# A spectral transform and two MLPs on one core: y's partial sums added as they leave PSUM, the first MLP's drain and the second MLP's first block laid out by hand

## The chip, the cores and the metric

The kernel runs on one core of one Trainium2 chip. The metric is device time in microseconds (us) of one execution, the median of three runs. The engines are named as in the profile: PE is TensorE (matmuls; PEld its weight loads), DVE is VectorE, ACT is ScalarE, POOL is GpSimd, SP is SyncE, whose queue issues every transfer here. Each engine works through its own queue in order; semaphores order the engines among each other.

## The reference, cut to what matters

```python
def reference(x, moe_w_in, moe_w_out, moe2_w_in, moe2_w_out):
    # x: (2, 3008, 256); w_in: (256, 2048); w_out: (2048, 256)
    y = np.fft.fft(np.fft.fft(x, axis=1), axis=2).real.astype(np.float32).reshape(6016, 256)
    r = np.maximum(y @ moe_w_in, 0.0)                  # first MLP
    y = ((r * r) @ moe_w_out).astype(np.float32)
    h = y @ moe2_w_in                                  # second MLP
    g = h * (1.0 / (1.0 + np.exp(-1.702 * h)))
    return (g @ moe2_w_out).astype(np.float32)
```

The weights come as 64-bit floats.

## The kernel before

**Numbers in two parts.** A float32 operand of a matmul is split into a high part (a cast to fp32r) and a low part (the operand less its high part), and a product is made of three matmuls: high by high, high by low, low by high. So nearly every operand costs one cast on ACT and one subtraction (the helper `sub`, line 78) on DVE or POOL. A 64-bit weight is narrowed to 32 bits first: `narrow` (from line 165) is six operations for a group of 1024 columns, two on ACT (lines 171, 174 or their like) and four on DVE (lines 175, 176, 185, 187).

**First stage.** x is folded by symmetry, transformed along the features and along the tokens, and stands as eight blocks j = 0 to 7 of 376 or 378 columns; a column is a pair of tokens, and each block has an even and an odd part.

**First MLP.** It runs in 128 steps i, listed in `steps`; a step is one block j and one slice f of 128 of the 2048 hidden features. `turns` gives the order: blocks 0, 1 and 2 are made in several turns, because the weights are narrowed meanwhile (block 0 in slices 0 to 4 and 4 to 16, block 1 in 0 to 4, 4 to 12 and 12 to 16, block 2 in 0 to 8 and 8 to 16), blocks 3 to 7 in one turn of 16. In a step `front1` makes six matmuls into a tile of the pool `psa` (two banks, two buffers). DVE turns them into h (lines 742, 744, 745: p, then two halves of h), ACT does relu, square and the cast to gh (lines 751, 752, 754), and POOL, in some steps DVE, subtracts gl a step later (line 78). The tile h has the tag "h" with four buffers. Four steps later (`LAG`) `back` multiplies gh and gl by the second weights: twelve matmuls, six for each output half ec = 0, 1, into the accumulators `acc[j]`, two tiles of the pool `psb`, which has just two buffers. At a turn's last step `store` copies both accumulators out, ec 0 on ACT and ec 1 on DVE (line 582), into tiles o that also have the tag "h", and sends them to a DRAM tile of that turn (line 583). So blocks 0, 1 and 2 leave two or three partial sums of y in DRAM. Outside of the parts written under `manual_schedule`, a scheduler in the compiler sets the order of each engine's queue from the program's order, so the order in the trace is not line by line that of the source.

Beside the steps run jobs of a plan (`PLAN`, `background`): the later parts of the transform, the narrowing of the weights, and at the end "y0" (from step 111, due at 128). That is `y_first`: `add_y(0)` loads the further partial sums of the first 512 columns and adds them on DVE (line 638), `sums_y` makes four differences of y's quarters (line 647), and `stage_a` and `stage_b` split y and these into yA and yB (ACT casts at line 654, DVE subtractions at line 78). yA may use a weight buffer that is free from step 117, yB one that is free from step 121.

**Second MLP.** y stands in six blocks of 512 columns (the last has 452), and a block is made in eight units p, so units u = 0 to 47. A unit multiplies by a two-by-two scheme with seven products: `products` (line 792) makes yb and ya's four into the PSUM tiles ab and cd, then, after DVE and ACT have formed u and g[3] from them (lines 839, 842, 843, 844), yc's three into the same tiles. DVE adds (line 868), ACT applies the activation (lines 867, 869) and casts gh a unit later (line 847), DVE subtracts gl. Two units later `back2` (line 808) multiplies by the output weights, half of it (ec 0) between the unit's first and second products, half (ec 1) after them. Its accumulators are `psb` tiles too. All of this is written under `manual_schedule`: the order of each engine's queue is the order of the source.

In units 0 and 1 the place of `back2` is taken by the drain: the last four steps' `back` (`drain`), two a unit. At u = 2 `leave` (lines 811 to 814) copies block 7's accumulators out, ec 0 on ACT and ec 1 on DVE, both through the one buffer of the tag "o" in the pool m3. Meanwhile a generator, `w2_late` (`rest`), is advanced by a number of pieces at three places in a unit. It narrows the last four groups of the second MLP's weights (input weights of group 2, output weights of group 2, then group 3 of each), loads y's block 1, adds its partial sums on DVE (`add_y(1)`) and makes its differences on DVE. For input weights `widen_in` makes four sums on POOL (line 234), four casts on ACT (line 242) and four subtractions on POOL (line 78). All narrowing goes through one buffer (`temp(cv2)`), the tile ue.

Input weights of group 2 are needed from u = 4, output weights of group 2 from u = 6, the next input group from u = 6, the next output group from u = 8. At the last unit of a block (`turn`) the next block's yB, yA and yC are made. At the very end the last accumulator leaves by two copies and two transfers (lines 891 to 896), again through the one buffer "o".

## Time and profile before

| what | value |
|---|---|
| three timed runs, us | 1013.51, 1017.29, 1017.41 (median 1017.29) |
| the profiled execution, us | 1017.06, of which the span from first to last instruction is 1015.3 |
| busy share of the span | PE 96%, weight loads 85%, DVE 70%, ACT 59%, POOL 32% |
| mean granted TensorE clock | 0.987 of full speed |
| end of the first MLP's last step on PE | 483.1 us after the span's start |
| first block of the second MLP (u = 0 to 7) | 483.1 to 590.9 us |

The profile is one execution. Its page gives shares of the whole span; what a stage is worth is read from its stretch: the busy time of each engine there, the clock that was granted, and which wait ended last before an engine went on. The rows below are in this form: a timeline row has the start, the duration, the engine, the line, the operation, the tile written and the tiles read, and in brackets how long the engine had stood idle before and what ended that.

### The profile page before, as it was taken

What the parts mean: (1) busy time and instruction counts of PE and PEld (TensorE: products, weight loads), DVE (VectorE), ACT (ScalarE), POOL (GpSimd) and SP (SyncE); (2) the same over time, 40 slices, a digit from 0 to 9 for tenths busy, and PEclk for the clock granted to TensorE, in tenths of its full rate; (3) what the DMA queues carried; (4) which work ended last, traced back from release to release, by engine and by line L of the source; (5) the groups of instructions that cost most, each with busy time, mean ns of one, the idle gap of its engine ahead of it and who ended that gap; (6) DMA issues with size and microseconds to landing.
All of it is one profiled execution on the core that took longest, in us unless ns stands there. A gap on an engine that the chain in (4) does not pass through costs nothing.

```text
span 1015.3 us, 12479 instructions
## 1 busy us (share of the span) xinstructions
PE 971.1 (96%) x4862; PEld 857.9 (85%) x4862; DVE 707.3 (70%) x881; ACT 599.7 (59%) x688; POOL 320.4 (32%) x200
## 2 busy tenths in 40 slices
PE   9889988999999999999779899999999999999997
PEld 8579988998999899999657688888888888888896
DVE  6996887885978787878656776575565556556552
ACT  2588887766676668787645454454454445445442
POOL 2367687534575457665223002020001001000000
PEclk9999999999999999999889999999999999999999
DMA  7640221300101001120211202002002000000101
GB/s 291 212 156 36 92 95 42 103 29 27 42 32 42 31 8 66 42 84 1 83 48 67 83 25 87 1 1 83 0 1 78 1 1 21 21 0 1 42 1 37
DMA packets 23675, 53.58 MB, mean 53 GB/s; under 512 B 3776, under 2 KB 17216, under 8 KB 20928
## 3 DMA queue, kind: packets, MB, share of 16 engines
q1 hardware_dynamic: 23616, 52.79, 15.1%
q8 instruction: 38, 0.62, 0.2%
q14 instruction: 21, 0.17, 0.1%
HBM read 37.36 MB, written 15.42 MB: 52 GB/s over the span
## 4 chain that ended last, share of the span: by engine, by line
PE 67%; DVE 7%; ACT 3%; issue 1%; DMA 1%; POOL 1%; DVEq 0%; ACTq 0%
PE psb L808 24%; PE psc L792 21%; PE psb L469 14%; PE psa L454 2%; PE psa L456 2%; PE psa L455 2%; PE psa L353 1%; POOL w2i L78 1%; DVE gl L78 1%; DVE h L744 1%; DVE ue L647 1%; DVE p L742 1%; DVE h L745 1%; DVE ue L185 1%; DMA ydram<-o 0%
## 5 line engine op out<-in xcount | busy, mean ns | idle before, releaser
L78 POOL TENSOR_TENSOR gl<-h,gh 128x752 fp32r<-128x752 f32 (+1 forms) x118 | 222.8, 1892 | 161.2 <-ACT gh L754 129.2
L469 PE MATMUL psb<-gh,w 128*128 128x376 f32 (+1 forms) x1024 | 239.2, 336 | 0.7 <-DVE o L582 0.7
L808 PE MATMUL psb<-gh,w 128*128 128x512 f32 (+1 forms) x768 | 223.5, 393 | 5.8 <-ACT o L813 5.8
L469 PEld LDWEIGHTS psb<-gh,w 128*128 128x128 f32 x1024 | 183.2, 189 | 1.9 <-issue 1.0
L808 PEld LDWEIGHTS psb<-gh,w 128*128 128x128 f32 x768 | 146.0, 190 | 36.7 <-ACT o L813 6.2
L868 DVE TENSOR_TENSOR g<-u,psc 128x1024 f32<-128x1024 f32 (+1 forms) x48 | 57.6, 1200 | 123.7 <-PE psc L792 123.7
L751 ACT ACTIVATE h<-h 128x752 f32<-128x752 f32 (+1 forms) x114 | 94.8, 832 | 65.3 <-DVE h L745 61.4
L469 PE MATMUL psb<-gl,w 128*128 128x376 f32 (+1 forms) x512 | 130.5, 336 | 0.0
L869 ACT ACTIVATE g<-g 128x1536 f32<-128x1536 f32 (+1 forms) x48 | 70.4, 1467 | 98.1 <-DVE g L868 98.1
L754 ACT CAST gh<-h 128x752 fp32r<-128x752 f32 (+1 forms) x128 | 105.0, 822 | 31.6 <-DVE h L749 24.7
L808 PE MATMUL psb<-gl,w 128*128 128x512 f32 (+1 forms) x384 | 121.0, 397 | 2.6 <-DVE gl L78 2.6
L792 PE MATMUL psc<-yc,w2i 128*128 128x512 f32 (+1 forms) x432 | 106.3, 389 | 4.3 <-DVE u L842 2.7
L78 DVE TENSOR_TENSOR gl<-g,gh 128x2048 fp32r<-128x2048 f32 (+1 forms) x48 | 108.8, 2266 | 2.1 <-ACT gh L847 1.2
L742 DVE SCALAR_TENSOR_TENSOR p<-n,w1n_t,psa 128x376 f32<-128x376 f32 (+1 forms) x128 | 76.4, 600 | 37.1 <-PE psa L456 36.6
L792 PEld LDWEIGHTS psc<-yc,w2i 128*128 128x128 f32 x432 | 80.6, 188 | 23.4 <-DVE u L842 4.3
L752 ACT ACTIVATE h<-h 128x752 f32<-128x752 f32 (+1 forms) x114 | 94.9, 834 | 3.1
L647 POOL TENSOR_TENSOR ue<-raw 128x512 f32<-128x512 f32 (+1 forms) x8 | 9.9, 1263 | 270.7 <-DVE yc L78 200.4
L454 PE MATMUL psa<-eo,w 128*128 128x376 f32 (+1 forms) x256 | 88.4, 346 | 6.6 <-DVE p L742 3.4
L469 PEld LDWEIGHTS psb<-gl,w 128*128 128x128 f32 x512 | 93.2, 190 | 0.0
L847 ACT CAST gh<-g 128x2048 fp32r<-128x2048 f32 (+1 forms) x48 | 90.1, 1876 | 0.1
L808 PEld LDWEIGHTS psb<-gl,w 128*128 128x128 f32 x384 | 72.6, 190 | 19.2 <-DVE gl L78 4.2
L455 PE MATMUL psa<-eo,w 128*128 128x376 f32 (+1 forms) x256 | 85.9, 336 | 0.0
(126 smaller groups left out, 1373.0 us busy)
## 6 DMA issues: line engine op xcount, KB each, us to landing
ydram<-o SPq DMA_DIRECT2D x18, 376.0 KB, 2.9
xt<-in_x SPq DMA_DIRECT2D x5, 1024.0 KB, 5.7
out<-o SPq DMA_DIRECT2D x10, 512.0 KB, 2.6
cst<-in_dfts SPq DMA_DIRECT2D x8, 570.0 KB, 5.6
raw<-in_w1i SPq DMA_DIRECT2D x4, 1024.0 KB, 4.9
raw<-in_w1o SPq DMA_DIRECT2D x4, 1024.0 KB, 6.2
raw<-in_w2i SPq DMA_DIRECT2D x4, 1024.0 KB, 4.9
raw<-in_w2o SPq DMA_DIRECT2D x4, 1024.0 KB, 5.0
```

What stands on the lines that cost most here:

```text
L78: eng.tensor_tensor(out=o, in0=a, in1=f32(b), op=ALU.subtract)
L454: T.matmul(o, lhsT=w[:, 0, fs], rhs=t[:, par, 0, 0:wd], start=True, stop=False)
L455: T.matmul(o, lhsT=w[:, 0, fs], rhs=t[:, par, 1, 0:wd], start=False, stop=False)
L469: T.matmul(acc[j][ec][:, s, 0:wd], lhsT=w[:, hl, e0:e0 + P], rhs=(gh, gl)[gi][:, s, 0:wd], start=(first and hl == 0 and gi == 0), stop=(la ...
L742: V.scalar_tensor_tensor(out=p[:, 0:wd], in0=e128[blocks[j]][:, 0:wd], scalar=w1n_t[:, 0, f:f + 1], in1=ps[:, 0, 0:wd], op0=ALU.mult, op1= ...
L751: A.activation(out=hv, in_=hv, func=AF.Relu)
L752: A.activation(out=hv, in_=hv, func=AF.Square)
L754: last_a = A.copy(gh[:, :, 0:wd], hv)
L792: T.matmul(bank, lhsT=w[:, hl, slot * P:(slot + 1) * P], rhs=x[:, yl, 0:wd], start=(first and hl == 0 and yl == 0), stop=(hl == 1), skip_g ...
L808: T.matmul(o[:, s, 0:wd], lhsT=w[:, hl, e0:e0 + P], rhs=g[:, 2 * i + s, 0:wd], start=(f == 0 and hl == 0 and g is gh), stop=(f == 15 and h ...
L847: A.copy(gh, gs[u - 1])
L869: A.activation(out=g[:, 1:4], in_=g[:, 1:4], func=AF.Gelu_apprx_sigmoid)
```

## The change

- `store` adds: where an earlier turn's sum of the block exists, the new function `ahead`, called one step before, loads it into two tiles o of the tag "h", DVE adds the accumulator onto each, and the sum goes out. So each block has one y in DRAM. `add_y` is removed, and `load_y` always reads one tensor a block; y's blocks after the first all come to raw buffer 1.
- `y_first` begins with `sums_y`. The differences of block 1 are made on POOL instead of DVE.
- The drain is halved by output: unit 0 makes ec 0 of all four last steps, unit 1 makes ec 1. Block 7's ec 0 leaves at u = 1 into a buffer of its own (`spare`), its ec 1 at u = 2.
- `w2_late` no longer is a generator: its pieces are put into a table by unit and place in the unit (0, 1 and 2 before yc's products, "m" between the two activations), and `do_late` issues them. The low halves of the input weights are made on DVE, the output weights are narrowed in a buffer of their own, and the last output group's narrowed weights go to raw buffer 0.
- The last output leaves through a buffer of the tag "g", and a small tile "edge" is allocated that nothing uses.

```diff
@@ -456,13 +456,13 @@
             T.matmul(o, lhsT=w[:, 1, fs], rhs=t[:, par, 0, 0:wd], start=False, stop=True)
         return pq
 
-    def back(j, f, first, last):
+    def back(j, f, first, last, ecs=range(2)):
         wd = WID[blocks[j][1]]
         if first:
             acc[j] = [ps_b(), ps_b()]
-        gh, gl = gst.pop((j, f))
+        gh, gl = gst[j, f]
         w = weights[0, 1, f // 4]
-        for ec in range(2):
+        for ec in ecs:
             e0 = (f % 4) * 256 + ec * P
             for hl, gi in ((0, 0), (0, 1), (1, 0)):
                 for s in range(2):
@@ -571,16 +571,30 @@
                     gone.add(name)
             assert name in gone, name
 
+    leaving = {}
+
+    def ahead(j):
+
+        wd = WID[blocks[j][1]]
+        leaving[j] = [m.tile([P, 2, NP], F32, tag="h", name="o", bufs=4) for _ in range(2)]
+        for ec, o in enumerate(leaving[j]):
+            nc.sync.dma_start(o[:, :, 0:wd], ydram[j][:, ec, :, 0:wd])
+
     def store(j, f):
 
         wd = WID[blocks[j][1]]
+        before = j in ydram
         y = dram.tile([P, 2, 2, NP], F32, tag=f"y{j}_{f}", name="ydram")
-        ydram.setdefault(j, []).append(y)
+        ydram[j] = y
+        o2 = leaving.pop(j, None)
         for ec in range(2):
-            o = m.tile([P, 2, NP], F32, tag="h", name="o", bufs=4)
             ap = acc[j][ec][:, :, 0:wd]
-            (A.copy, V.tensor_copy)[ec](o[:, :, 0:wd], ap)
-            nc.sync.dma_start(y[:, ec, :, 0:wd], o[:, :, 0:wd])
+            o = (o2[ec] if before else m.tile([P, 2, NP], F32, tag="h", name="o", bufs=4))[:, :, 0:wd]
+            if before:
+                V.tensor_tensor(out=o, in0=o, in1=ap, op=ALU.add)
+            else:
+                (A.copy, V.tensor_copy)[ec](o, ap)
+            nc.sync.dma_start(y[:, ec, :, 0:wd], o)
 
     pend = None
     n = len(steps)
@@ -602,40 +616,9 @@
         return tl[:, 0:4 * NP2].rearrange("p (e s k) -> p e s k", e=2, s=2)
 
     def load_y(m):
-        yr[m] = f32(quarters(raw_tile(m % 2)))
+        yr[m] = f32(quarters(raw_tile(1 if m else 0)))
         for j, lo, hi, at in pieces(m):
-            nc.sync.dma_start(yr[m][:, :, :, at:at + hi - lo], ydram[j][0][:, :, :, lo:hi])
-
-    def add_y(m):
...
     def sums_y(m, eng):
         wd = WID2[m]
@@ -678,23 +661,11 @@
             else:
                 yield from widen(1, 1, g, cv2, dest, then=then)
 
-    def w2_late():
-        then = ((lambda: load_w(1, *order[6], slot=1)), (lambda: load_w(1, *order[7], slot=0)), (lambda: load_y(1)), None)
-        yield lambda: load_w(1, *order[5], slot=0)
-        for i in range(4):
-            k, g = order[4 + i]
-            if k == 0:
-                yield from widen_in(g, temp(cv2), (winp, wq), then=then[i])
-            else:
-                yield from widen(1, 1, g, cv2, (winp, wq)[g - 2], then=then[i])
-        yield from y_next(1)
-
     def until(i):
         while at_step[0] < i:
             yield lambda: None
 
     def y_first():
-        yield from add_y(0)
         yield from sums_y(0, V)
         yield from until(117)
         yA[0] = view(winp.tile([P, 2, 1024], F32R, tag="w", name="ya"), 2)
@@ -704,12 +675,90 @@
         yield from stage_b(0)
 
     def y_next(m):
-        if m > 1:
-            load_y(m)
-            yield lambda: None
-            yield lambda: None
-        yield from add_y(m)
-        yield from sums_y(m, G if m > 1 else V)
+        load_y(m)
+        yield lambda: None
+        yield lambda: None
+        yield from sums_y(m, G)
+
+    late = {}
+
+    def put(u, spot, *items):
+        late.setdefault((u, spot), []).extend(items)
+
+    def in_parts(g, ue, tiles):
...
+        return sums, highs, lows
+
+    def out_parts(g, u, w):
+        weights[1, 1, g] = w
+        return lambda: A.copy(w[:, 0], u), lambda: sub(V, w[:, 1], u, w[:, 0])
+
+    def w_tile(pool, dtype=F32R):
+        return pool.tile([P, 2, 1024], dtype, tag="w", name="w2")
+
+    def w2_late():
+
+        load_w(1, *order[5], slot=0)
+        in2, spare, out2, in3 = (w_tile(winp), w_tile(wq)), w_tile(wq, F32), w_tile(winp), (w_tile(winp), w_tile(wq))
+        ue = temp(cv2)
+        p = list(narrow(raws[1, 0, 2], ue, (1, 0, 2)))
+        sums, highs, lows = in_parts(2, ue, in2)
+        put(0, 1, *p, lambda: load_w(1, *order[6], slot=1), *sums)
+        put(1, 1, *highs, *lows)
+
+        def out_2():
+            p = list(narrow(raws[1, 1, 2], spare, (1, 1, 2)))
+            put(1, "m", *p[:2])
+            put(2, 1, *p[2:], lambda: load_w(1, *order[7], slot=0))
+            put(3, 1, *out_parts(2, spare[:, 0], out2))
+
+        def in_3():
+            ue = temp(cv2)
+            p = list(narrow(raws[1, 0, 3], ue, (1, 0, 3)))
+            sums, highs, lows = in_parts(3, ue, in3)
+            p[0]()
+            p[1]()
+            put(3, 1, *p[2:5], lambda: load_y(1))
+            put(4, 1, p[5], *sums)
+            put(5, 1, *highs, *lows)
+
+        def out_3():
+            p = list(narrow(raws[1, 1, 3], spare, (1, 1, 3)))
+            for item in p[:4]:
+                item()
+            put(5, 0, p[4])
+            put(6, 1, p[5])
+
+        def out_3_end():
+            high, low = out_parts(3, spare[:, 0], raw_tile(0, F32R).rearrange("p (h c) -> p h c", h=2))
+            high()
+            put(7, 1, low)
+
+        put(1, 0, out_2)
+        put(2, 2, in_3)
+        put(4, 2, out_3)
+        put(6, 1, lambda: run(sums_y(1, G)))
+        put(6, "m", out_3_end)
+        return spare
+
+    def do_late(u, spot):
+        for f in late.get((u, spot), ()):
+            f()
 
     held = []
     by_hand = ExitStack()
@@ -726,6 +775,8 @@
             zp.release()
             w2b = tc.alloc_tile_pool(name="w2b", bufs=3, side="left", reuse_waits="tile")
         at_step[0] = i
+        if LAG <= i + 1 < n and steps[i + 1 - LAG][4] and steps[i + 1 - LAG][1] in ydram:
+            ahead(steps[i + 1 - LAG][1])
         j, f = steps[i][1:3]
         ps = front1(j, f)
         done = steps[i - LAG][1:] if i >= LAG else None
@@ -781,7 +832,8 @@
     yC[0] = m2.tile([P, 2, 3, NP2], F32R, tag="yc", name="yc")
     units = 8 * BLKS
     run(stage_c(0))
-    rest = w2_late()
+    rest = None
+    spare = w2_late()
     drain = [steps[n - LAG + k][1:] for k in range(LAG)]
     gs, gsp = {}, {}
 
@@ -808,8 +860,9 @@
                     T.matmul(o[:, s, 0:wd], lhsT=w[:, hl, e0:e0 + P], rhs=g[:, 2 * i + s, 0:wd],
                              start=(f == 0 and hl == 0 and g is gh), stop=(f == 15 and hl == 1), skip_group_check=True)
 
-    def leave(wd, src, ec, dst):
-        o = m3.tile([P, 2, NP2], F32, tag="o", name="o")
+    def leave(wd, src, ec, dst, o=None):
+        if o is None:
+            o = m3.tile([P, 2, NP2], F32, tag="o", name="o")
         (A.copy, V.tensor_copy)[ec](o[:, :, 0:wd], src[:, :, 0:wd])
         nc.sync.dma_start(dst[:, :, 0:wd], o[:, :, 0:wd])
 
@@ -828,10 +881,11 @@
                 products(cd[:, 0], True, (S1, yA[0][:, :, 0]))
                 products(cd[:, 1], True, (S3, yA[0][:, :, 1]))
 
+            if u == 1:
+                ydram[7] = dram.tile([P, 2, 2, NP], F32, tag="y7_15", name="ydram")
+                leave(WID[3], acc[7][0], 0, ydram[7][:, 0], spare[:, 0].rearrange("p (s k) -> p s k", s=2))
             if u == 2:
-                ydram[7] = [dram.tile([P, 2, 2, NP], F32, tag="y7_15", name="ydram")]
-                for ec in range(2):
-                    leave(WID[3], acc[7][ec], ec, ydram[7][0][:, ec])
+                leave(WID[3], acc[7][1], 1, ydram[7][:, 1])
             if t > 0 and t % 8 == 0:
                 leave(WID2[t // 8 - 1], acc["2", t // 8 - 1][1], 1, out[t // 8 - 1, 1])
             if here:
@@ -846,19 +900,21 @@
                 gh = (m3, m2)[(u - 1) % 2 == 0].tile([P, 4, NP2], F32R, tag="gh", name="gh")[:, :, 0:pw]
                 A.copy(gh, gs[u - 1])
             if u < 2:
-                back(*drain[2 * u])
+                for d in drain[0:2]:
+                    back(*d, ecs=(u,))
             elif t < units:
                 back2(t, 0)
                 if t % 8 == 7:
                     leave(WID2[t // 8], acc["2", t // 8][0], 0, out[t // 8, 0])
             if here:
                 turn = p == 7 and j < BLKS - 1
-                if rest is not None and not run(rest, 3 if j == 0 else 2):
+                do_late(u, 0)
+                do_late(u, 1)
+                do_late(u, 2)
+                if rest is not None and not run(rest, 2):
                     rest = None
                 if turn:
-                    if rest is not None:
-                        run(rest)
-                        rest = None
+                    assert rest is None
                     run(stage_b(j + 1))
                     run(stage_a(j + 1))
                 products(ab[:, 0], False, (A12, yC[0][:, :, 0]))
@@ -866,12 +922,12 @@
                 products(cd[:, 1], False, (A22, yC[0][:, :, 2]))
                 A.activation(out=g[:, 0], in_=ab[:, 0], func=AF.Gelu_apprx_sigmoid)
                 V.tensor_tensor(out=g[:, 1:3], in0=v.unsqueeze(1).to_broadcast([P, 2, wd]), in1=cd, op=ALU.add)
+                do_late(u, "m")
                 A.activation(out=g[:, 1:4], in_=g[:, 1:4], func=AF.Gelu_apprx_sigmoid)
                 gs[u] = g
-                if j == 0 and rest is not None and not run(rest, 2):
-                    rest = None
             if u < 2:
-                back(*drain[2 * u + 1])
+                for d in drain[2:4]:
+                    back(*d, ecs=(u,))
                 if u == 1:
                     mg.release()
                     m3 = tc.alloc_tile_pool(name="m3", bufs=1, side="right", reuse_waits="tile")
@@ -881,14 +937,13 @@
                 gl = m3.tile([P, 4, NP2], F32R, tag="gl", name="gl", bufs=2)[:, :, 0:pw]
                 sub(V, gl, gs[u - 1], gh)
                 gsp[u - 1] = (gh, gl)
-            if here and j == 0 and rest is not None and not run(rest, 3):
-                rest = None
             if here and turn:
                 run(stage_c(j + 1))
                 if j < BLKS - 2:
                     rest = y_next(j + 2)
 
-        o = m3.tile([P, 2, NP2], F32, tag="o", name="o")
+        m3.tile([P, 8], F32, tag="edge", name="edge")
+        o = m2.tile([P, 4, NP2], F32, tag="g", name="o", bufs=2)
         wd = WID2[-1]
         A.copy(o[:, 0, 0:wd], acc["2", BLKS - 1][1][:, 0, 0:wd])
         nc.sync.dma_start(out[BLKS - 1, 1, :, 0, 0:wd], o[:, 0, 0:wd])
```

## Rows read from the trace of the kernel before

**Rows 1.** The page, busy time and share of the span by engine, instructions.

```profile
PE 971.1 (96%) x4862; PEld 857.9 (85%) x4862; DVE 707.3 (70%) x881; ACT 599.7 (59%) x688; POOL 320.4 (32%) x200
```

**Rows 2.** Busy time by stretch: per engine us (count), then granted clock, DMA share, GB/s.

```profile
483.10:590.90 107.80, 89.05 (x363) 70.11 (x362) 71.80 (x77) 56.49 (x62) 21.22 (x18) 0.92 0.22 71
590.90:673.90 83.00, 83.00 (x362) 67.53 (x361) 51.88 (x49) 41.08 (x39) 5.09 (x4) 1.00 0.09 28
483.10:500.60 17.50, 11.23 (x47) 9.30 (x46) 10.11 (x13) 10.88 (x14) 3.58 (x2) 0.80 0.18 60
500.60:509.60 9.00, 9.00 (x48) 8.13 (x47) 6.25 (x7) 4.54 (x5) 2.97 (x4) 1.00 0.33 117
509.60:530.50 20.90, 13.56 (x46) 9.80 (x45) 9.00 (x10) 9.71 (x12) 5.33 (x4) 0.84 0.11 38
565.90:580.50 14.60, 12.21 (x47) 9.58 (x46) 10.37 (x11) 6.49 (x6) 0.00 (x0) 0.88 0.34 106
```

**Rows 3.** Timeline of PE, 480 to 580: start, us, line, output<-inputs, [idle before <-releaser].

```profile
482.79 0.51 PE L469 MATMUL psb<-gh,w 128*128 128x376 f32 x2
488.39 0.79 PE L792 MATMUL psc<-yb,w2i 128*128 128x512 f32 x1 [5.10 <-ACT yb L654]
500.64 1.52 PE L792 MATMUL psc<-yb,w2i 128*128 128x512 f32 x6
503.36 0.51 PE L469 MATMUL psb<-gh,w 128*128 128x376 f32 x2
518.25 1.22 PE L808 MATMUL psb<-gh,w 128*128 128x512 f32 x2 [5.78 <-ACT o L813]
537.32 0.97 PE L792 MATMUL psc<-yc,w2i 128*128 128x512 f32 x3 [0.88 <-DVE u L842]
571.67 0.97 PE L808 MATMUL psb<-gl,w 128*128 128x512 f32 x2 [2.39 <-DVE gl L78]
```

**Rows 4.** Timeline of DVE, same columns.

```profile
481.48 2.05 DVE L78 TENSOR_TENSOR ya<-ue,ya 128x1024 fp32r<-128x1024 f32 x1 [1.98 <-ACT ya L654]
483.46 0.59 DVE L742 SCALAR_TENSOR_TENSOR p<-n,w1n_t,psa 128x376 f32<-128x376 f32 x1
488.37 1.93 DVE L78 TENSOR_TENSOR yb<-raw,yb 128x512 fp32r<-128x512 f32 x1 [3.19 <-ACT yb L654]
490.83 1.21 DVE L78 TENSOR_TENSOR yc<-raw,yc 128x1024 fp32r<-128x1024 f32 x1
523.17 0.94 DVE L813 COPY o<-psb 128x752 f32<-128x752 f32 x1 [11.05 <-DMA ydram<-o]
524.03 0.68 DVE L842 TENSOR_TENSOR u<-a,psc 128x512 f32<-128x512 f32 x1
```

**Rows 5.** Timeline of ACT, same columns.

```profile
487.00 0.82 ACT L754 CAST gh<-h 128x752 fp32r<-128x752 f32 x1
516.41 1.12 ACT L171 ACTIVATE ue<-raw 128x1024 f32<-128x1024 f32 x1 [4.09 <-POOL w2i L78]
```

**Rows 6.** Timeline of POOL, same columns.

```profile
487.95 1.80 POOL L78 TENSOR_TENSOR gl<-h,gh 128x752 fp32r<-128x752 f32 x1 [2.14 <-ACT gh L754]
511.05 5.33 POOL L78 TENSOR_TENSOR w2i<-ue,w2i 128x512 fp32r<-128x512 f32 x4 [3.99 <-ACT w2i L242]
```

**Rows 7.** Timeline of the last microseconds, PE and ACT.

```profile
1008.25 0.57 PE L808 MATMUL psb<-gh,w 128*128 128x452 f32 x2
1010.63 0.54 ACT L893 COPY o<-psb 128x452 f32<-128x452 f32 x1 [3.33 <-DMA out<-o]
```

**Rows 8.** The tile o: one operation's ns min/median/max, and transfers from issue to landing.

```profile
L582 DVE COPY o<-psb x11: 928/941/945, 73.7 to 447.7; 128x752 f32<-128x752 f32 x8, 128x756 f32<-128x756 f32 x3
DMA to landing us min/median/max: 2.1/2.9/7.5
```

**Rows 9.** Timeline of PE and POOL beside the second store of block 1.

```profile
139.20 0.44 PE L454 MATMUL psa<-eo,w 128*128 128x378 f32 x1 [2.04 <-DVE p L742]
138.03 6.26 POOL L78 TENSOR_TENSOR gl<-h,gh 128x756 fp32r<-128x756 f32 x3
```

44 lines of the change are left out of this document (17 added, 27 removed).

## The prediction

> **What bounds the kernel now.** I read the page first: TensorE (PE) is busy for 971 us of a span of 1015.3 [rows 1], so only two things can make this kernel much shorter: fewer matmuls, or fewer microseconds in which PE stands still or runs at its lower clock. The change takes no matmul away. So I looked for PE's idle time, with the table of busy time by stretch. The last product of the first MLP's steps ends at 483.1 us [rows 3]. From 590.9 us on PE has no gap: eight units of the second MLP take exactly 83.0 us there, all busy at a granted clock of 1.00, which is 10.375 us a unit [rows 2]. Between these times, in the first MLP's drain and the second MLP's first block (units u = 0 to 7), 107.8 us pass with 89 us of PE busy and a mean granted clock of 0.92 [rows 2]. Units 0 and 1 hold narrower matmuls; u = 1 has no gap and takes 9.0 us [rows 2]. The stretch without a stall would therefore be 2 x 9.0 + 6 x 10.375 = 80.25 us, and the loss is 107.8 - 80.25 = **27.55 us**. That is the stake. By unit: 17.5 - 9.0 = 8.5 in u = 0, 20.9 - 10.4 = 10.5 in u = 2, 14.6 - 10.4 = 4.2 in u = 6 [rows 2], and 4.3 spread over u = 3 to 5.
>
> Then the timelines say what ended each gap. u = 0: the last two products of the first MLP's steps start at 482.79 and the next matmul at 488.39, after 5.10 us of waiting for ya and yb [rows 3]. These are late because DVE makes y's sums first: it subtracts ya at 481.48 and only then, at 483.46, starts on the last step of the first MLP, so that gh of that step ends at 487.8 [rows 4, 5] and yb's subtraction follows at 488.37. u = 2: PE waits 5.78 us for PSUM that holds the last sums of the first MLP [rows 3]. ACT could not copy them out because it stood 4.09 us in front of a narrowing step, which waited for POOL's low halves (5.33 us) to leave the buffer [rows 5, 6]; then DVE waited 11.05 us to copy the other half, because both copies share one buffer and the first had to reach memory [rows 4]. u = 6: 2.39 us for gl, behind a late low half on DVE [rows 3]. The waits are dear twice over: after 5.10, 5.78 and 2.39 us of idling PE runs at 1.2 GHz for a while (granted clock 0.80, 0.84, 0.88 over these units [rows 2]).
>
> **The change part by part.** The sum is made against the profiled execution, 1017.06 us, of which 1015.3 are the span; the median of the three timed runs is 1017.29, so no correction is needed.
>
> *y's sums move to the store.* Blocks 0 to 2 of the first MLP are made in two or three turns; four stores (steps 27, 39, 43, 51) are a second or third one. There the change loads the earlier part a step ahead into two of the four "h" buffers, and DVE adds PSUM onto them. DVE pays one operation where ACT had a copy; a DVE copy of that shape takes 941 ns [rows 8], and I take the add to cost the same, 0.95. ACT gets its copy back. What matters is the ring of four buffers: two are held over a step, so the next h waits for a POOL subtraction two steps back instead of four, and the one after the store waits for the transfer out, 2.9 us from issue to landing, at most 7.5 [rows 8]. A step of PE takes about 3.1 us (18 products; the 24 narrow ones of u = 1 take 9.0 - 21 x 0.227 = 4.2 us, 0.175 each [rows 2, 3]), and PE has two sets of psa banks, so about one late step is absorbed. At step 27 POOL already lags by three subtractions, 6.26 us, and PE already loses 2.04 us there [rows 9]. So each store costs PE between a gain of 0.7 (ACT is freer) and about 2.5 (5.6 us of lateness, landing plus the add and a lag, less 3.1 of slack). I take 0.6 each, nearer to the lower end since stores 39 to 51 cost PE almost nothing now: **+2.5 us, range -3 to +10**. Eight loads come onto SP's queue, all long before they are used but two steps from what follows them; the loads and adds in the first MLP's last steps and in the second MLP's first three blocks go. Those adds lay on DVE beside PE work except in the last steps, and that gain is in the next item.
>
> *u = 0.* Without the adds, stages a and b of block 0 are done when their buffers allow it, at steps 117 to 121, some 20 us before the drain. Then DVE starts the last step as soon as its products are there, 481.2 (the last back product group ends at 483.13 and its twelve matmuls take 2.07). Following the durations before: h at 482.9, gh (three ACT passes, 2.6) 485.5, POOL's gl 485.6 to 487.4 [rows 6]. PE goes on at 483.13 without a gap. But yc is still made after gh: two ACT casts to 487.1, then two DVE subtractions. DVE's yb took 1.93 us beside POOL's gl, where half of yc's 1.21 would be expected [rows 4, 6]; so yc's first subtraction ends at 488.5, its second at 489.1, and u and two adds of 0.7 [rows 4] follow at 489.9, 490.6 and 491.3. PE has done the first products (2.72, from two starts in rows 3) and half of the drain (2.1) by 487.95, waits 1.95 us for u, and after 0.7 us of work 0.7 more: **2.65 us remain** of 8.5. If the lower clock follows, 1.7 us more: after 2.39 us of idling it did [rows 3], after 0.88 it did not [rows 3]; I take half, 0.9.
>
> *The drain halved by output, and the exits of block 7.* All of ec 0 is now finished in u = 0 and leaves in u = 1 to a buffer of its own; ec 1 leaves in u = 2. ACT's copy no longer stands behind a narrowing step, DVE's no longer behind a transfer, and PE needs the banks only in u = 2. The 10.5 us of u = 2 go to nothing. The matmuls are the same in number.
>
> *The narrowed weights.* Low halves of the input weights go from POOL to DVE, sums of y's block 1 from DVE to POOL, and each piece gets its place, so that no ACT step comes before the buffer it needs is free. What is late next is DVE, busy 71.8 us in this stretch [rows 2], which would shrink to some 85: four adds and four sums leave it, some ten low pieces come, so it would be about 85% busy. I expect one wait of the kind seen in u = 3, 0.88 [rows 3] and a shorter one right behind it, in u = 1, where a copy, gh and the high halves queue on ACT: **1.4 us**. Bounds for u = 1 to 7: 0 to 13 (half of the present loss). The spare buffer is read by the transfer of ec 0 when narrowing wants it; at a landing of 2.9 that is past, at 7.5 it would hold ACT about 2 us, which the 10 us unit hides.
>
> *The last output.* Its two copies get a buffer that no transfer holds. PE ends at 1008.82, ACT's copy starts only at 1010.63 after 3.33 us of waiting [rows 7]; it could start at 1008.9: **-1.7 us**. The two copies and the last transfer behind it stay.
>
> Sum: 1017.06 - 27.55 + 2.65 + 0.9 + 1.4 + 2.5 - 1.7 = **995.3 us**.
>
> **The rivals.** (1) *Waits change place in the first block.* ACT and DVE are strictly in order and the layout has no slack of its own; if one piece is a microsecond later than I walked it, a PE wait returns. With half the loss still there (13.8 in place of 4.95): 1004 us. For it: DVE at 85%. Against: PE has gaps now only where a buffer or a bank was held, and these are removed. (2) *A held port.* DVE's subtraction of two SBUF tiles waited for POOL's to end (1.93 us at 488.37 to 490.3; POOL's ended at 489.75 [rows 4, 6]). After the change twelve POOL sums lie in the first block beside DVE's gl and low halves; if each holds DVE for 1.2 us, that is 14 us of DVE, of which some 12 are free and the rest, with gl late a few times, costs PE about 5: 1000 us. The Trainium skill states this rule ("SBUF — State Buffer", section "SBUF: two separate sides"): GpSimd shares a port pair with VectorE under an exclusive lock, and whichever starts first holds it for its whole instruction. By that rule the low halves on DVE are safe once POOL has finished its sums, and y's sums on POOL beside DVE's gl are not; the trace agrees with the lock at 488.37. (3) *The ring of h buffers.* If each of the four stores costs PE 2.5 us: 1003 us. (4) *The same ring, on the slower side.* If the transfers land in 7.5 us and POOL is three subtractions behind each time, as at step 27, DVE waits 7.5 + 6.3 - 3.1 = 10.7 us a store, 43 us in all: 1036 us. It decides against the change from about 6 us of PE per store (24.3 / 4). Against it: only one of the four stores shows such a lag now. (5) *The change doesn't do what it says*: ya and yb are still late, because the order of the first MLP's last steps is again set by DVE; then u = 0 keeps its 8.5 in place of 3.55, and the time is 1000 us.
>
> **How the numbers follow.** Forecast 995 us with chance 0.60; rival 1 0.13, rival 2 0.08, rival 3 0.08, rival 5 0.05, rival 4 and its milder forms 0.06. The low end: everything fits (1 us left in u = 0 to 7) and the stores gain 3: 1017.06 - 27.55 + 1 - 3 - 1.7 = 986. The high end takes in rivals 1, 2, 3 and 5: 1005. A measurement tells 0.5%, 5 us, from no change. Faster by more than that is everything but rival 4: 0.91; within it 0.04; slower 0.05.
>
> **What would show it right or wrong.** Right: in the table by stretch, the eight units take 82 to 87 us instead of 107.8 and the clock stays at or near 1.00; no PE wait on ACT's yb, on o, or on gl in u = 6; a wait on DVE's u right after the drain's first half. At the end ACT's last copy follows the last matmul at once. Wrong: PE idle beside the four stores, at 140 to 235 us, with DVE waiting there for POOL's gl or for the transfer of o; or new PE waits on w2i or on gl in u = 1 to 7; or DVE waiting for POOL beside the sums.

## The result, and the profile after

The changed kernel takes 985.55 us, median of four runs (984.19 to 986.55), against 1015.84 for four runs of the kernel before (1013.51 to 1017.41): a ratio of 0.9703, 95% interval 0.9677 to 0.9729. The forecast was 995; the time lies just below the low end of its range, 986. The profiled execution took 984.19, of which 982.4 are the span.

The page, by engine, answers [rows 1]: PE's work is the same in number and 13.5 us shorter.

```profile
PE 957.6 (97%) x4862; PEld 855.0 (87%) x4862; DVE 699.9 (71%) x879; ACT 596.9 (61%) x684; POOL 325.7 (33%) x196
```

Busy time by stretch, columns as in [rows 2]. The first two rows are the first block of the second MLP and the eight units after it; then u = 0, 1 and 2.

```profile
482.90:565.30 82.40, 79.94 (x362) 66.56 (x361) 67.95 (x71) 54.52 (x59) 18.61 (x14) 1.00 0.18 61
565.30:646.90 81.60, 81.60 (x362) 67.59 (x361) 50.12 (x47) 40.28 (x39) 7.15 (x4) 1.00 0.08 26
482.90:494.30 11.40, 9.51 (x47) 7.97 (x46) 8.10 (x9) 8.03 (x10) 2.77 (x2) 1.00 0.31 98
494.30:504.10 9.80, 9.22 (x47) 7.87 (x46) 6.75 (x10) 8.44 (x11) 2.95 (x4) 1.00 0.38 140
504.10:514.30 10.20, 10.20 (x47) 8.48 (x46) 9.71 (x10) 6.76 (x7) 0.00 (x0) 1.00 0.22 63
```

The first block went from 107.8 to 82.4 us and runs at a granted clock of 1.00 instead of 0.92. But look at the second row: eight units that had no gap before took 83.0 us [rows 2] and take 81.6 now. That is 10.20 us a unit instead of 10.375, where PE waits for nothing in either kernel.

PE's timeline at the joint, columns as in [rows 3]:

```profile
482.67 0.51 PE L469 MATMUL psb<-gh,w 128*128 128x376 f32 x2
483.02 1.54 PE L844 MATMUL psc<-yb,w2i 128*128 128x512 f32 x6
489.30 0.97 PE L844 MATMUL psc<-yc,w2i 128*128 128x512 f32 x3 [1.34 <-DVE u L896]
490.82 1.65 PE L844 MATMUL psc<-yc,w2i 128*128 128x512 f32 x6 [0.55 <-DVE g L898]
494.38 1.54 PE L844 MATMUL psc<-yb,w2i 128*128 128x512 f32 x6
500.62 1.65 PE L844 MATMUL psc<-yc,w2i 128*128 128x512 f32 x6 [0.57 <-DVE g L898]
504.18 1.53 PE L844 MATMUL psc<-yb,w2i 128*128 128x512 f32 x6
```

Three waits, 2.46 us in all, are what remains; the waits of 5.10, 5.78 and 2.39 us of [rows 3] are gone. DVE, the tile o (first its add, between 60 and 470 us, then its transfers), and the last microseconds, to compare with [rows 4], [rows 8] and [rows 7]:

```profile
486.00 2.05 DVE L78 TENSOR_TENSOR yc<-raw,yc 128x1024 fp32r<-128x1024 f32 x1 [3.63 <-ACT yc L637]
506.59 0.93 DVE L866 COPY o<-psb 128x752 f32<-128x752 f32 x1
```

```profile
L594 DVE TENSOR_TENSOR o<-o,psb x8: 931/932/943, 134.8 to 224.7; 128x752 f32<-128x752 f32 x6, 128x756 f32<-128x756 f32 x2
DMA to landing us min/median/max: 2.3/3.0/7.6
```

```profile
977.29 0.57 PE L860 MATMUL psb<-gh,raw 128*128 128x452 f32 x2
977.90 0.54 ACT L948 COPY o<-psb 128x452 f32<-128x452 f32 x1 [1.56 <-PE psb L860]
```

DVE's copy of block 7's second half waits for no transfer (it waited 11.05), and ACT's last copy starts 0.04 us after the last matmul's end at 977.86.

Where the 32.9 us between the two profiled executions went:

| part | before | after | change |
|---|---|---|---|
| to the end of the first MLP's steps | 483.1 | 483.0 | -0.1 |
| first block (u = 0 to 7) | 107.8 | 82.4 | -25.4 |
| u = 8 to the last matmul's end (1008.82; 977.86) | 417.9 | 412.5 | -5.4 |
| from there to the end of the span | 6.5 | 4.5 | -2.0 |

The third line had no term in the forecast. Two things had to be found out: what makes a matmul shorter, and which part of the change is worth what in the first block.

### The profile page after: what moved, and what is told of

It is laid out like the page before. It is cut to its first block, busy times and chain, and to the rows that moved or that the text cites. A ratio compares the mean times of both kernels' runs of the same rounds, so it can differ in the third digit from the quotient of the medians.

```text
span 982.4 us, 12467 instructions
## 1 busy us (share of the span) xinstructions
PE 957.6 (97%) x4862; PEld 855.0 (87%) x4862; DVE 699.9 (71%) x879; ACT 596.9 (61%) x684; POOL 325.7 (33%) x196
## 4 chain that ended last, share of the span: by engine, by line
PE 81%; DVE 10%; ACT 4%; issue 3%; POOL 1%; DMA 1%; SPq 0%; DVEq 0%; ACTq 0%; POOLq 0%
PE psb L860 26%; PE psc L844 22%; PE psb L469 20%; PE psa L454 3%; PE psa L455 3%; PE psa L456 3%; PE psa L353 2%; DVE p L793 1%; ACT h L802 1%; ACT h L803 1%; DVE h L796 1%; DVE h L795 1%; ACT gh L805 1%; POOL gl L78 1%; DVE ue L630 1%
## 5 line engine op out<-in xcount | busy, mean ns | idle before, releaser
L469 PEld LDWEIGHTS psb<-gh,w 128*128 128x128 f32 x1024 | 183.1, 189 | 0.9 <-DVE o L596 0.5
L860 PE MATMUL psb<-gh,w 128*128 128x512 f32 (+1 forms) x576 | 163.7, 386 | 0.0
L860 PEld LDWEIGHTS psb<-gh,w 128*128 128x128 f32 x576 | 108.1, 188 | 20.5
L630 POOL TENSOR_TENSOR ue<-raw 128x512 f32<-128x512 f32 (+1 forms) x10 | 22.7, 2295 | 252.9 <-DMA raw<-ydram 246.5
L454 PE MATMUL psa<-eo,w 128*128 128x376 f32 (+1 forms) x256 | 88.2, 345 | 9.6 <-DVE h L796 5.7
L469 PEld LDWEIGHTS psb<-gl,w 128*128 128x128 f32 x512 | 93.0, 189 | 0.0
L860 PE MATMUL psb<-gl,w 128*128 128x512 f32 (+1 forms) x288 | 87.7, 386 | 0.0
L795 DVE TENSOR_TENSOR h<-p,psa 128x376 f32<-128x376 f32 (+1 forms) x128 | 69.9, 546 | 24.1 <-POOL gl L78 11.0
L456 PE MATMUL psa<-eo,w 128*128 128x376 f32 (+1 forms) x256 | 85.8, 336 | 0.0
L455 PE MATMUL psa<-eo,w 128*128 128x376 f32 (+1 forms) x256 | 85.8, 336 | 0.0
L923 ACT ACTIVATE g<-psc 128x512 f32<-128x512 f32 (+1 forms) x48 | 28.3, 590 | 76.6 <-PE psc L844 76.6
```

The costliest lines, as they stand in the source:

```text
L454: T.matmul(o, lhsT=w[:, 0, fs], rhs=t[:, par, 0, 0:wd], start=True, stop=False)
L455: T.matmul(o, lhsT=w[:, 0, fs], rhs=t[:, par, 1, 0:wd], start=False, stop=False)
L456: T.matmul(o, lhsT=w[:, 1, fs], rhs=t[:, par, 0, 0:wd], start=False, stop=True)
L469: T.matmul(acc[j][ec][:, s, 0:wd], lhsT=w[:, hl, e0:e0 + P], rhs=(gh, gl)[gi][:, s, 0:wd], start=(first and hl == 0 and gi == 0), stop=(la ...
L860: T.matmul(o[:, s, 0:wd], lhsT=w[:, hl, e0:e0 + P], rhs=g[:, 2 * i + s, 0:wd], start=(f == 0 and hl == 0 and g is gh), stop=(f == 15 and h ...
```

## The experiments

Six kernels (e2_edge64, e4_edge288, d2_move_both, s1_store_alone, u1_undo_drain, u2_undo_layout) were executed once, so their times have no interval. The runs were made on several chips, each beside the kernel before, whose medians there lie between 1013.7 and 1017.3 us; by its time alone, a difference of two or three microseconds between kernels that did not run side by side is not shown.

### What made the unit shorter: 32 bytes

No line of the change touches the units u = 8 to 39. What it does touch is the place of their operands: the tile `edge`, 32 bytes a partition, stands in the pool m3 ahead of gl and of every other unit's gh. The allocator's addresses (bytes within a partition) show gl at 200672 before and at 200640 after; the weights stay at 17856, 26048 and so on, all of them multiples of 8192 apart. First the tile alone was taken from the changed kernel, then it alone was put into the kernel before, then its size was doubled.

```diff
-        m3.tile([P, 8], F32, tag="edge", name="edge")
```

> The changed kernel without the small tile 'edge', so that the pool m3 (gl, one of the two gh, o) lies 32 bytes higher, as in the kernel before (gl at byte 200672 of a partition instead of 200640); every instruction and its order stay. Theory A, the address theory: the units of the second MLP got shorter (10.375 to 10.20 us) because these tiles now start at a multiple of 64 bytes. Then the units from u = 8 on go back to about 10.37 us, and the time rises by 46 x 0.17 = 8 us, to about 993.5. Theory B, the rhythm theory: they got shorter because of what no longer runs beside PE (y's adds, the exits); then units stay at 10.20 and the time at 985.5.

> The kernel before with the one line of the small tile 'edge' added and nothing else. Theory A: the units from u = 8 on take 10.20 instead of 10.375 us, the first block keeps its stalls, and the time falls by about 46 x 0.17 = 8 us, to 1008 (ratio to before 0.992). Theory B: no change, 1016.

> The changed kernel with an 'edge' of 64 bytes instead of 32: m3's tiles move another 32 bytes down (gl at 200608), to 32 past a multiple of 64. Theory A (the address modulo 64): units of 10.37 us, about 993.5 us in all, as without the edge. If any shift away from the old place does it (a neighbour, a conflict with one other tile): 10.20 and 985.5. Theory B: 10.20 as well.

Without the edge 992.13 us (ratio to before 0.976, 0.9744 to 0.9776), 6.6 more than the changed kernel. The kernel before with the edge: 1011.26 (0.9942, 0.9919 to 0.9965), 4.6 less than the 1015.88 beside it. With 64 bytes 991.9, as without any. So the tile that I called unused is worth some 5 to 7 us. The matmuls on gl between 600 and 860 us, duration in ns as min/median/max, in the kernel before, the changed kernel, without the edge, and before with the edge:

```profile
L808 PE MATMUL psb<-gl,w x202: 393/396/399, 600.3 to 859.9; 128*128 128x512 f32 x101
```

```profile
L860 PE MATMUL psb<-gl,w x156: 389/389/389, 600.5 to 859.1; 128*128 128x512 f32 x156
```

```profile
L860 PE MATMUL psb<-gl,w x152: 393/396/399, 603.2 to 858.7; 128*128 128x512 f32 x152
```

```profile
L808 PE MATMUL psb<-gl,w x204: 389/389/390, 600.8 to 857.4; 128*128 128x512 f32 x102
```

Is it an address that is a multiple of 64 bytes, or of 128? Three kernels moved the first MLP's gh, gl and eo (rows of 384 instead of 378 numbers) and with them the left side, the weights among it:

```diff
-        gh = mg.tile([P, 2, NP], F32R, tag="gh", name="gh", bufs=5)
+        gh = mg.tile([P, 2, 384], F32R, tag="gh", name="gh", bufs=5)
```

(the same for gl and eo; small tiles are put into other buffers to make room, and in a2_align128 and a3_align512 a row of the transform's table is two numbers shorter, so that the weights stand 448, 384 and 512 bytes lower.)

> The changed kernel with the first MLP's moving operands (gh, gl, eo) also at multiples of 64 bytes: 384 columns a row instead of 378, and the pool moved; to make room, four small tiles of the start lie in buffers of h and p. In the changed kernel's trace those matmuls of 376 columns start 0.166 to 0.176 us apart, 0.1725 in the mean, while the aligned ones of 512 are 0.2267 nearly throughout. Theory A: the spread is that of aligned and not aligned operands, the mean falls to about 0.168, and 1536 + 768 matmuls gain 0.004 each, 10 us: 976. If the rule holds only for tiles of 512 columns or only for their base and not for the rows inside, less: 980 to 985. Theory B: no gain, 985 plus or minus what another order of the first stage brings.

> As a1_align, but all of the left side lies 64 bytes higher, so that weights and moving operands of both MLPs have the same address modulo 128 (64 past a multiple). In the four traces so far a matmul of the second MLP starts 0.2267 us after the last where its moving operand and its weights agree modulo 128, and 0.230 to 0.236 where they differ by 32, 64 or 96; in a1_align the weights had moved by 64 against gl and one gh, and its units fell back to 10.36. Theory A128 (the difference between the moving operand's address and the weights' counts, modulo 128): units of 10.20 us again, and the first MLP's matmuls, 0.1725 us in the mean now, become even and come down to about 0.170, 2304 x 0.0025 = 6 us: about 979. Theory A64 (the moving operand's address modulo 64 counts, and a1's units were slow for another reason, as the small tiles moved): units as slow as in a1_align, 983 to 984.

> As a1 and a2, with all weights and moving operands of both MLPs at the same address modulo 512 (448 past a multiple, rows of gh, gl and eo 1536 bytes). What the runs leave over: m3's tiles lie from the weights at 10752 = 21 x 512 in the changed kernel (even 0.2267 us a matmul), and at 32, 480, 448 and 384 modulo 512 in the kernel before, e2, a1 and a2 (0.224 to 0.238); a difference of 0 modulo 128 (a2) was not enough. Theory A512: units of 10.20 us, and the first MLP's matmuls of 376 columns come to an even 0.170, from 0.1727: 2304 x 0.0027 = 6 us, about 979. If only the second MLP's follow (units 10.20, first MLP as before): 985.

983.81 us (0.9678, 0.966 to 0.9695), 984.36 (0.9693, 0.9666 to 0.9721), 981.84 (0.9676, 0.965 to 0.9702). All three are at or a little under the changed kernel, but not for the reason I had: in the first two the second MLP's units are slow again, 10.36 and 10.33 us on average, though gl stands at 200640 in both, as in the changed kernel. So neither a multiple of 64 or 128 nor the place of gl decides. What differs between the three is the distance to the weights. Three more kernels tested that: one with an edge longer by 256 bytes, then a pair that holds either gl or the distance and moves the other (lines of the three edits put together).

```diff
+    small.tile([P, 8], F32, name="pad")            # d1_move_left, d2_move_both: left side 32 bytes up
-        m3.tile([P, 8], F32, tag="edge", name="edge")   # d1_move_left alone
+        m3.tile([P, 72], F32, tag="edge", name="edge")  # e4_edge288 alone
```

> The changed kernel with an 'edge' of 288 bytes: m3's tiles lie 256 modulo 512 from the weights. Theory A512 (512 is the period): units of 10.3 to 10.4 us, 992. If the period is 256: 10.20, 985.5.

> The kernel after without the edge tile, but with 32 bytes put ahead of the tiles on the left side, the weights among them: gl and gh of the second MLP stand where they stood in the kernel before (gl at 200672), the weights are 32 bytes further up, and the distance between the two is the same as in the kernel after, modulo 256 bytes. Theory 'distance' (what counts is how far a matmul's moving operand stands from its weights, modulo 256 bytes): units of 10.20 us, as in the kernel after, and 984 to 987 us. Theory 'place' (what counts is where the moving operand itself stands): units of 10.33 to 10.41 us, as without the edge, and 991 to 993 us.

> The kernel after with its edge tile kept, and 32 bytes put ahead of the tiles on the left side: gl and gh stand exactly where they stand in the kernel after (gl at 200640), and the distance to the weights is 32 bytes less, 224 modulo 256. Theory 'distance': units over 10.29 us and 990 to 993 us. Theory 'place': units of 10.20 us and 984 to 987 us.

e4_edge288: 986.16. d1_move_left: 985.52 (0.9697, 0.9673 to 0.972), with gl exactly where it stood in the kernel before. d2_move_both: 992.01, with gl exactly where it stands in the changed kernel. First d1_move_left, then d2_move_both, the same group:

```profile
L861 PE MATMUL psb<-gl,w x156: 389/389/389, 600.6 to 857.2; 128*128 128x512 f32 x156
```

```profile
L861 PE MATMUL psb<-gl,w x152: 395/396/397, 602.6 to 857.4; 128*128 128x512 f32 x152
```

Place is refuted, distance holds. The kernels that differ in it, in one table (distance from the first weight tile to gl, modulo 256; unit from the starts of the matmuls, mean of odd and even units):

| kernels | distance mod 256 | gl matmul, ns | unit, us |
|---|---|---|---|
| before, e1_no_edge | 32 | 393/396/399 | 10.37 |
| after, e3_before_edge, e4_edge288, d1_move_left, a3_align512, f1_align_near (below) | 0 | 389/389/389 (390 once) | 10.20 |
| e2_edge64, d2_move_both | 224 | 395/396/397 | 10.35 |
| a1_align | 192 | 393/394/394 | 10.36 |
| a2_align128 | 128 | 387/394/398 | 10.33 |

Equal distances give equal rows, wherever the tiles lie. Distances of 0 and 256 modulo 512 do alike and 128 does not, which fits a period of 256 bytes. A third reading, that the distance between one moving operand and the next counts, falls by the kernel before: in every other unit there gh as well as gl lies in m3, at 221152 and 208864, a multiple of 256 apart, and the matmuls on both still start every 231 to 236 ns, while in the units between, with gh at 189888, a multiple of 256 from the weights, those on gh ahead of gl start every 227. That it is the weights and no other tile of the left side is likely but not shown, since that side moved as a whole in every edit. Why the distance matters is not shown either: no row names a wait.

The rule does not reach the first MLP. In a3_align512 all its moving operands (gh, gl and eo) stand a multiple of 256 bytes from their weights as well, where in the changed kernel the distances are scattered; yet its matmuls of 376 columns start every 173.3 ns on average (260 to 460 us) against 172.3 in the changed kernel and 171.8 in a1_align, whose distances there are 64 and 192. So the 6 us that was expected of them did not come. The matmuls on gl there, the changed kernel and a3_align512:

```profile
L469 PE MATMUL psb<-gl,w x242: 328/335/342, 260.6 to 459.7; 128*128 128x376 f32 x89, 128*128 128x378 f32 x32
L469 PE MATMUL psb<-gl,w x244: 332/334/339, 260.2 to 458.5; 128*128 128x376 f32 x90, 128*128 128x378 f32 x32
```

### The parts of the change, one at a time

```diff
@@ u1_undo_drain: the changed kernel, but
-                for d in drain[0:2]:
-                    back(*d, ecs=(u,))
+                back(*drain[2 * u])
...
-            if u == 1:
+            if u == 2:
+                for ec in range(2):
+                    leave(WID[3], acc[7][ec], ec, ydram[7][:, ec])
```

s1_store_alone is the kernel before with `ahead`, the new `store` and no `add_y`; u2_undo_layout is the changed kernel with the late weights in the old generator's order instead of the table.

> The kernel before with only the sums at the store: 'ahead' and the adds in 'store', no add_y; drain, exits, late weights and the last output as before, and m3 at its old place. Theory as predicted: ya and yb are ready before the drain, so u = 0 loses 2 to 4 us instead of 8.5; the stalls of u = 2 to 6 stay (18 us), units stay 10.37; at step 27 the ring of h costs PE a wait of 4 to 5 us in place of 2.7. Sum 1016 - 5 + 2, about 1010 to 1012. Rival (it is the drain's other order that cured u = 0): u = 0 keeps its 8.5, 1016 to 1020.

> The changed kernel with the drain by steps again (both output halves of two steps a unit) and both exits at u = 2 through the one buffer o. Theory as predicted: the wait of DVE for the first exit's transfer comes back, about 5 us, and PE waits for the banks and for u in u = 2 for some 3 to 6 us; the rest of the first block stays as in the changed kernel: 989 to 992. Rival (the order of the late weights alone had cured u = 2): under 1.5 us, 985 to 987.

> The changed kernel with the late weights in the old order: a generator advanced by 3, 2 and 3 pieces a unit, all narrowing through one buffer, the input weights' low halves on POOL, y's block 1 differences on DVE; drain, exits, store and last output as changed. Theory as predicted: the waits of u = 3, 5 and 6 come back (2.2, 1.9 and 4.2 us before) and ACT stands behind POOL's low halves in u = 1 or 2 for some 4 us, of which part reaches PE: 993 to 998. Rival (these stalls were only echoes of u = 2's): under 2 us, 985 to 988.

s1_store_alone took 1012.39 us, 4.1 less than the 1016.51 beside it: u = 0 falls from 17.5 to 11.4 us, while u = 2 keeps its loss (22.1 us, 20.9 before). u2_undo_layout took 1000.15, 14.6 more than the changed kernel. u1_undo_drain took 987.45: the drain halved by output and the separate exits are worth no more than 1.9, and in its trace 0.7 of the 2.0 us that u = 0 to 2 take longer are a lower clock in u = 0 that, as said below, is not the drain's. PE's waits from 480 to 590 us (engine, tile, line, releaser: us in all, times, the longest), s1_store_alone, u2_undo_layout and u1_undo_drain:

```profile
PE psb L791 <- ACT o L796: 5.8, 1, 5.8
PE psc L775 <- DVE u L825: 4.9, 4, 1.9
PE psb L791 <- DVE gl L78: 2.4, 1, 2.4
```

```profile
PE psc L822 <- DVE u L874: 6.8, 4, 3.7
PE psb L838 <- DVE gl L78: 2.5, 1, 2.5
```

```profile
PE psc L844 <- DVE u L895: 1.3, 1, 1.3
PE psc L844 <- DVE g L897: 1.1, 2, 0.5
```

With the old order and the new exits, the wait for o is gone, but u = 2 still takes 15.8 us: ACT stands 4.2 us before a narrowing step,

```profile
ACT ue L171 <- POOL w L78: 4.2, 1, 4.2
```

which is the wait of 4.09 us that stood ahead of o before [rows 5]; now it holds DVE's u instead. With the new order and the old exits, u = 2 takes 11.5: DVE waits 1.66 us for the shared buffer's transfer. Undone one at a time, the two cost 5.6 and 1.3 us of u = 2; together, in the kernel before, 10.5, where DVE's copy stood behind the transfer of an ACT copy that was itself late [rows 4, 5].

### The ring of h buffers

The waits that rival 4 spoke of came at one store, step 27. POOL, DVE and PE there in the changed kernel:

```profile
133.29 2.41 POOL L78 TENSOR_TENSOR w<-ue,w 128x1024 fp32r<-128x1024 f32 x1
135.78 2.36 POOL L279 TENSOR_TENSOR t<-xt 128x1024 f32<-128x1024 f32 x1
138.11 3.53 POOL L78 TENSOR_TENSOR gl<-h,gh 128x756 fp32r<-128x756 f32 x2
```

```profile
134.82 0.93 DVE L594 TENSOR_TENSOR o<-o,psb 128x752 f32<-128x752 f32 x1
139.92 0.55 DVE L795 TENSOR_TENSOR h<-p,psa 128x378 f32<-128x378 f32 x1 [4.17 <-POOL gl L78]
```

```profile
140.98 0.68 PE L454 MATMUL psa<-eo,w 128*128 128x378 f32 x1 [4.67 <-DVE h L796]
```

The subtractions for w and t ahead of gl (2.41 and 2.36 us) seemed to be all of it. s2_relieve_pool was to give both to DVE, b1_both the same in a3_align512, c1_align_low only the first there. The traces show that LOW (0, 0, 2) was the wrong entry: it is a subtraction at 81 us, and the one at 133 stayed on POOL in all three. So the first two moved the fold's subtraction, plus one at 81 us, and c1_align_low only the latter.

```diff
-LOW = {... (0, 0, 2): "G", ...}
+LOW = {... (0, 0, 2): "V", ...}
-                (V if q in (1, 2) else G).tensor_tensor(out=t[:, 1, a], ...
+                (V if q in (1, 2, 3) else G).tensor_tensor(out=t[:, 1, a], ...
```

> The changed kernel with two operations taken from POOL and given to DVE just ahead of step 27: the low half of the first MLP's input weights of group 2 (2.4 us on POOL) and the subtraction of the transform's part 3 (2.4 us). Theory (the ring of h at the store waits for POOL's backlog): the wait of 4.67 us of PE at 141 us falls below 1.5 us, no lower clock follows it, and the time falls by 3 to 5 us, to 981 to 982. Rival (the ring waits for the store's transfer, or DVE is the bound there): the wait stays at 4 us or moves to the next step, 985.

> a3_align512 and s2_relieve_pool together, a version meant to beat both kernels. By A512 and the ring theory 985.5 - 6 - 4 = 975.5; by either alone 979 to 982.

> a3_align512 with one of the two edits of s2_relieve_pool: the subtraction for the weights of LOW (0, 0, 2) on VectorE (1.2 us there) instead of GpSimd (2.41 us at 133.29 in the kernel after), and the fold's subtraction left on GpSimd. Theory 'the fold's 2.47 us on VectorE is what gave the gain back in s2_relieve_pool': the wait near 136 falls from 4.4 to 2 to 3 us, no new wait of 1.8 us comes near 156, and the time is 979 to 981.5 us against 981.84. Theory 'any work moved to VectorE in this stretch comes back as a wait': 982 to 986 us.

All three missed. s2_relieve_pool: 989.25 (0.975, 0.9726 to 0.9775), 3.7 above the changed kernel; b1_both 984.09 (0.9693, 0.9668 to 0.9717), 2.3 above a3_align512 with overlapping intervals; c1_align_low 981.67 (0.9656, 0.9627 to 0.9685), level with a3_align512, and its wait stayed 4.4 us. In s2_relieve_pool PE's wait near 136 did shrink, to 2.7 us. But the fold's subtraction now stands in DVE's queue, then the additions behind it, ahead of the h that PE needs:

```profile
151.54 2.47 DVE L279 TENSOR_TENSOR t<-xt 128x1024 f32<-128x1024 f32 x1
156.72 1.79 DVE L284 TENSOR_TENSOR xt<-t 128x512 f32<-128x512 f32 x1
158.44 0.54 DVE L795 TENSOR_TENSOR h<-p,psa 128x378 f32<-128x378 f32 x1
```

```profile
159.49 0.44 PE L454 MATMUL psa<-eo,w 128*128 128x378 f32 x1 [1.44 <-DVE h L796]
```

and further pauses follow, after which PE runs at a granted clock of 0.66 from 175 to 185 us.

### A version that beats both

a1_align's first MLP ended earliest (476 us), but its units were slow. f1_align_near adds 192 bytes to its edge, and nothing else:

```diff
-        m3.tile([P, 8], F32, tag="edge", name="edge")
+        m3.tile([P, 56], F32, tag="edge", name="edge")
```

> a1_align with the edge tile 192 bytes longer, so that the second MLP's gl and gh stand a whole multiple of 256 bytes from the weights (a1_align: 192 bytes off it); nothing else is changed. Theory 'distance': the matmuls on gl take 389 ns instead of 393 to 394, a unit 10.20 us instead of 10.36, and with a1_align's first MLP (its steps end near 476 us) the time is 983.81 less 38 units of 0.16 us: 977 to 978.5 us. Rival: the early end of a1_align's first MLP was that one execution's, and the time is 980 to 983 us. Rival 'place': units stay at 10.33 to 10.39 us and the time at 983 to 985 us.

977.96 us (977.1 to 979.13; ratio to before 0.9633, 0.9598 to 0.9667): 5.9 less than a1_align, and 7.6 less than the changed kernel. The row is the fast one again:

```profile
L860 PE MATMUL psb<-gl,w x156: 389/389/389, 600.3 to 859.6; 128*128 128x512 f32 x156
```

Its first MLP ends at 477.5. About half of that lead over the changed kernel (2.6 of 5.5 us) is there by 78 us, where the same matmul starts at 75.30 instead of 77.92; how much of it comes from the addresses and how much from the order of the first stage was not separated. One row that the longer rows do change is POOL's subtraction for gl, 1.67 us at the median (250 to 460 us) instead of 1.82; it does so in all of a1_align, a2_align128, a3_align512 and f1_align_near.

On this kernel the right entry was moved, alone:

```diff
-LOW = {... (0, 0, 3): "G", ...}
+LOW = {... (0, 0, 3): "V", ...}
```

> f1_align_near with the weight subtraction of LOW (0, 0, 3) on VectorE instead of GpSimd. This is the one of 2.43 us that stands ahead of gl at 130.0 us in f1_align_near (133.29 in the kernel after); s2_relieve_pool and c1_align_low had moved (0, 0, 2) by mistake, which stands at 81 us. Theory 'GpSimd's queue sets the wait at step 27': gl ends some 2.4 us earlier, PE's wait of 4.4 us there falls to 2 to 3 us, and the time is 976 to 977.5 us against 977.96. Theory 'work moved to VectorE in this stretch comes back as another wait', as the fold's subtraction did: 978 to 982 us.

978.14 us (976.9 to 979.72; 0.9648, 0.9629 to 0.9667): no change that the times show, though its profiled execution ended the first MLP at 475.8. POOL and PE at the ring:

```profile
131.28 2.38 POOL L279 TENSOR_TENSOR t<-xt 128x1024 f32<-128x1024 f32 x1 [1.80 <-DVE w L78]
133.61 3.28 POOL L78 TENSOR_TENSOR gl<-h,gh 128x756 fp32r<-128x756 f32 x2
```

```profile
136.36 0.68 PE L454 MATMUL psa<-eo,w 128*128 128x378 f32 x1 [3.34 <-DVE h L796]
```

POOL's 2.43 us are gone, but 1.80 of them come back as idle time until DVE's subtraction, now in their place, is done, so gl is only some 0.7 us earlier relative to what stands before it, and PE's wait falls from 4.4 to 3.3. That POOL's queue ahead of gl sets this wait is shown by its shrinking in both edits (to 2.7 and 3.3); that it can be had for nothing is not.

## Why the prediction was right or wrong

The direction and the places were right; the sum was 9.75 us too high against the median, and 11.1 against the profiled execution (995.3 - 984.19). By its own steps:

*The unit of 10.375 us: this step failed.* The prediction's "eight units of the second MLP take exactly 83.0 us there, all busy at a granted clock of 1.00, which is 10.375 us a unit" was taken as a floor that the change cannot move. It was no floor: within it each matmul on gl took 393 to 399 ns in place of 389. The tile edge, written down as unused, got no price. The term is -5.4 us after u = 7 and 6 x 0.175 = -1.05 in it, -6.5 in all; e1_no_edge measures 6.6, and its 992.13 lies inside the stated range. No range held the term, because a matmul's duration was not among the unknown costs. The trace of before held a hint: at one shape and one clock its matmuls on gl took 396 ns and those on ya 389,

```profile
L792 PE MATMUL psc<-ya,w2i x150: 389/389/393, 602.6 to 852.7; 128*128 128x512 f32 x150
```

and the prediction itself used 0.227 us for a matmul, of which a unit of 45 makes 10.2 us and not 10.375. The 11.1 us divide into 6.45 for the unit, 1.75 for the first block (4.95 less 3.2), 2.6 for the first MLP and 0.3 for the tail.

*u = 0 and u = 1.* Forecast 2.65 + 0.9 + 1.4 = 4.95 us over the narrow floor; now 82.4 - (2 x 9.0 + 6 x 10.20) = 3.2, of which 2.46 are the three waits. The waits fell on u and on g where they were foretold, but shorter, and the clock stayed at 1.00. The yc subtraction, foretold to end at 488.5, ended at 488.05. The lower clock that I gave half a chance came in u1_undo_drain after the same two pauses (1.3 and 0.5 us): there u = 0 took 12.9 us instead of 11.4. It came as well in e2_edge64, d1_move_left, d2_move_both and f1_align_near (12.8 to 13.0), whose drain is that of the changed kernel, so in 4 of the 15 traces with that drain; u = 1 then lost its wait, and both units together took some 0.7 us more.

*u = 2.* Its 10.5 us went to nothing, as forecast, but I gave them to the drain and the exits. The runs give most to the layout: 5.6 of u = 2 stay without it, 1.3 without the new drain and exits. The sum hid this, since both are in the change.

*u = 3 to 7.* No wait at all; the bounds for u = 1 to 7 were 0 to 13. DVE is 68.0 us busy of 82.4, 82%, where 85% was expected; that load did no harm, so rival 1 falls.

*The stores.* Forecast +2.5 with bounds -3 and +10. In the profiled execution the first MLP ends 0.1 us earlier than before. One pair of traces misleads here: the nine traces of kernels with the new store and the first MLP's gh, gl and eo in their old places end their steps at 483.0 to 485.6, on average 484.4; the two with the old store at 483.1 and 480.2. So +2.5 fits, but two traces that differ by 2.9 do not measure it; that the term read -0.1 in the pair above is luck. Nor is it four times 0.6: step 27 pays 4.67 us in place of 2.04 [rows 9] and 0.67, and the other three nothing; between the casts of gh of steps 24 and 30 the changed kernel falls 1.55 us behind the kernel before (130.55 to 155.48 against 130.41 to 153.79). The trace of before ran 20 us at a clock of 0.83 (165 to 185), which that of the changed kernel did not; this hid it. Rivals 3 and 4 were right in mechanism, at one store of four.

*The held port, rival 2.* yc's subtraction began at 486.00 and ended at 488.05, while POOL worked until 486.97; beyond that stand 1.08 us, about the 1.21 that such a subtraction took alone [rows 4]. The y sums on POOL, which rival 2 feared, took 1.2 to 1.3 us each, even beside DVE's additions that read PSUM, except the second of each block's four: it fell beside DVE's gl and took 3.2 to 3.4, and that gl took up to 3.01 where 2.29 is the median.

```profile
542.63 1.30 POOL L630 TENSOR_TENSOR ue<-raw 128x512 f32<-128x512 f32 x1 [6.35 <-DVE w L78]
543.61 2.48 DVE L78 TENSOR_TENSOR gl<-g,gh 128x2048 fp32r<-128x2048 f32 x1
543.89 3.34 POOL L630 TENSOR_TENSOR ue<-raw 128x512 f32<-128x512 f32 x1
```

This agrees with the lock that the Trainium skill states ("SBUF — State Buffer", section "SBUF: two separate sides"). Yet no PE wait came of it in the first block: gl grew by 0.2 to 0.7 us a block, not by the 1.2 a sum that rival 2 reckoned with, and what was lengthened had slack.

*The tail.* -1.7 forecast, -2.0 measured. *Rival 5* falls: no wait for ya or yb.
